# Writing out by hand the instruction order of a mixture of experts on three engines

## The chip, the cores and the metric

The kernel runs on one core of one Trainium2 chip. The metric is the device time of one execution in microseconds (us). A core has five engines that run side by side and wait for one another through semaphores: TensorE (PE in the profile; PEld are its weight loads), VectorE (DVE), ScalarE (ACT), GpSimd (POOL) and SyncE (SP). SP and POOL issue the data transfers here.

## The reference

Three layers follow one another on 2304 tokens of width 512: a windowed attention, a dense gated MLP, and a noisy top-2 mixture of 8 experts. The change touches the third alone:

```python
for e in range(E):                      # E = 8, F = 1024
    for k in range(2):
        mask = top2[:, k] == e
        h = np.maximum(x[mask] @ w1[e], 0.0)
        out[mask] += top2_w[mask, k, None] * (h @ w2[e])
```

## The kernel before

**Precision.** Every float32 operand of a large product is split into a high part (rounded to the matmul's type) and a low part (the rest). A product is three matmuls: high x high, high x low, low x high. A split is `Seven.split`: a copy on ScalarE writes the high part, then a subtraction on VectorE writes the low part. Weights come raw from HBM into one of three buffers `wst` and are split on the chip.

**An expert's tokens.** The tokens of an expert are 608 rows (`CW`) in 5 blocks (`CAP`). `gather(e, j)` fetches the rows of block j by an indirect DMA on POOL's queue into a tile `xo3` (two buffers). `gt(e, j, bank)` turns it with 4 transposes on TensorE; ScalarE copies the result into `xr`, and POOL copies the rows' weights into `wcol`.

**The first product** of experts 1 to 7 is `Seven.p1(e, i)` for i = 0 to 3, each for two of the 8 column blocks of `w1[e]`. It is a scheme of seven products (P1 to P7) on quarters of the operands instead of eight. `sums` makes four sums of quarters on VectorE (L1164 to L1167) and `operands(0..5)` split quarters and sums. Weights go through the same: `prep` takes the next job from the list `jobs`. A job ("w1", e, i) makes four differences on VectorE (L1142 to L1145) and four splits; a job ("w2", e, i) is one split of two column blocks of `w2[e]`. `load` issues the raw loads of the next jobs.

Each product is 6 matmuls (L1186). P1, P6 and P5 add up in one bank A. P1's result is needed alone as well, so ScalarE copies it to a bank B_ (L1199) before P6 may add to A; the copies C (L1203) and D_ (L1207) follow P6 and P5 in the same way, and `us` takes a copy of P7 (L1201). VectorE adds `us` to A (u0, L1208) and to C (u1, L1211). `out` finishes a quarter: an eviction with Relu on ScalarE (L1195), then its low part on VectorE (L1196).

**The second product** `p2(e, j)` is 24 matmuls (L315 to L317) for block j. VectorE then weights the result and adds it to the rows fetched from `out` by `prev(e, j)` (L970), and POOL scatters the rows back. Expert 0 is done by other functions, in part while the MLP still runs; the late half of its first product, `p1(0, f, (1,))` for 8 column blocks f (L932), and its blocks 3 and 4 of p2 stand at the start of this phase.

**What sets the order.** Instructions are written as a program; a scheduler orders them on each engine with a timeline of its own, by readiness and priority, and may move an instruction ahead of earlier ones. Within a region `tc.manual_schedule(engines=...)` the engines named issue in the order written; the others are left to the scheduler. Before, no such region covers the experts from `sv = Seven()` on.

Of the kernel before, what the change touches and what calls it, by code (L numbers as in the profile page):

```python
# [9 lines left out]
F32 = mybir.dt.float32  # L10
# [19 lines left out]
def tile_alibi_window_attention__swiglu__noisy_top2_moe(  # L30
# [33 lines left out]
    CAP = 5  # L64
# [13 lines left out]
    def bank(i):  # L78
        return psum.tile([128, 512], F32, name=f"b{i}", tag=f"b{i}")
# [222 lines left out]
    def place1(n):  # L302
        return main.tile([128, 2, 2, NU], F32R, name="wu", bufs=3)
# [594 lines left out]
    def gather(e, j):  # L898
        g = j >= EARLY
        if e == 0 and e not in XG:  # L900
            XG[e] = new_xt(e)
        x = wpool[3].tile([128, RW], F32, name="xo3", bufs=2) if e else wpool[1].tile([128, RW], F32, name="xo", bufs=2)
        GB[e, j] = x
        col = e * SB + j
        r = nrow(j)
        nc.gpsimd.indirect_dma_start(out=x[0:r], out_offset=None,  # L906
                                     in_=x2d[0:GRP[-1][0], :] if (e, g) == (0, False) else x2d,
                                     in_offset=bass.IndirectOffsetOnAxis(ap=R["g"][0:r, col:col + 1], axis=0))

    def gt(e, j, t):  # L910
        x, r = GB[e, j], nrow(j)
        for c in range(KC):
            nc.tensor.transpose(t[:, c * 128:c * 128 + r], x[0:r, c * 128:(c + 1) * 128], ident[0:r, 0:r])  # L913
        tv = t.rearrange("p (c s) -> p c s", c=KC)[:, :, 0:r]
        if e:
            nc.scalar.activation(sv.xr[:, :, j * 128:j * 128 + r], tv, AF.Copy)
        else:
            d = [XG[e][:, s, :].rearrange("p (c s) -> p c s", c=KC)[:, :, j * 128:j * 128 + r] for s in range(2)]
            nc.scalar.activation(d[0], tv, AF.Copy)
            nc.vector.tensor_sub(d[1], tv, f32(d[0]))  # L920
        nc.gpsimd.tensor_copy(wcol[0:r, e * CAP + j:e * CAP + j + 1], x[0:r, DM + e:DM + e + 1])
# [147 lines left out]
    class Seven:  # L1069
# [3 lines left out]
        def __init__(self):  # L1073
            self.xr = wpool[3].tile([128, KC, CW], F32, name="xr")
            n = 2 * HS
            s = wpool[3].tile([128, 4 * n], F32, name="xs")
            self.s = [s[:, i * n:(i + 1) * n].rearrange("p (c t) -> p c t", c=2) for i in range(4)]
            u = wpool[3].tile([128, 2 * HS], F32, name="us")
            self.u = [u[:, 0:HS], u[:, HS:]]
            self.t = hB[:, PB * DM:PB * DM + 1024].rearrange("p (o k f) -> p o k f", o=4, k=2)  # L1080
            z = NF2 * CW
            self.wb = [([hT[:, i, z:z + 512] for i in range(2)], [hT[:, i, z + 512:z + 768] for i in range(2)])]
            self.wa, self.w2, self.w2t = [], {}, None
            self.jobs = []
            for e in range(1, E):
                self.jobs += [("w1", e, i) for i in range(4)] + [("w2", e, i) for i in range(4)]
            self.jobs = ([j for j in self.jobs if j[:2] == ("w1", 1)][:3] +
                         [j for e in range(1, E) for j in
                          [("w1", e, 3)] + [("w2", e, i) for i in range(4)] + [("w1", e + 1, i) for i in range(3) if e + 1 < E]])
            self.nl = self.nj = 0  # L1090
            self.raw = {}

        def open(self):
# [34 lines left out]
            p, b = self.wb[i % 3]  # L1128
            return a, [x.rearrange("p (o k f) -> p o k f", o=2, k=2) for x in p], [x.rearrange("p (k f) -> p k f", k=2) for x in b]

        def prep(self, n=1):
            for _ in range(n):
                if self.nj == len(self.jobs):
                    return
                self.load(self.nj + 1)
                what, e, i = self.jobs[self.nj]
                r = self.raw.pop(self.nj)
                self.nj += 1
                if what == "w1":
                    a, b, c = w = self.w1_operands((e - 1) * 4 + i)  # L1140
                    t = self.t
                    nc.vector.tensor_sub(t[:, 0], r[:, 0:2, 1], r[:, 0:2, 0])  # L1142
                    nc.vector.tensor_sub(t[:, 1], r[:, 2:4, 1], t[:, 0])
                    nc.vector.tensor_sub(t[:, 2], r[:, 2:4, 1], r[:, 0:2, 1])
                    nc.vector.tensor_sub(t[:, 3], r[:, 2:4, 0], t[:, 1])  # L1145
                    self.split([a[:, s, 0:2].rearrange("p o k f -> p (o k) f") for s in range(2)], r[:, :, 0])
                    self.split([a[:, s, 2:4] for s in range(2)], t[:, 0:2])
                    self.split(b, t[:, 2:4])
                    self.split(c, r[:, 2:4, 1])
                    self.w2["w1", e, i] = w  # L1150
                else:
                    if i < 3:
                        t = place1(0)
                    else:
                        t = self.w2t
                    self.split([t[:, :, s, :] for s in range(2)], r)
                    for u in range(2):
                        self.w2[e, 2 * i + u] = t[:, u]
                self.load(self.nj + 2)

        def sums(self):
            x, s = self.xr, self.s
# [26 lines left out]
        def p1(self, e, i):  # L1189
            A, Z, B_, C, D_ = (bank(x)[:, 0:HS] for x in ((6, 7, 0, 1, 4), (2, 3, 5, 6, 7), (0, 1, 2, 3, 4), (5, 6, 7, 0, 1))[i])  # L1190
            lo, hi = slice(0, HS), slice(HS, CW)

            def out(ps, f, sl):
                d = h2[0][:, f, sl]
                nc.scalar.activation(d, ps, AF.Relu)  # L1195
                nc.vector.scalar_tensor_tensor(h2[1][:, f, sl], ps, 0.0, f32(d), op0=OP.max, op1=OP.subtract)  # L1196

            self.product(e, i, "P1", A, True)
            nc.scalar.activation(B_, A, AF.Copy)  # L1199
            self.product(e, i, "P7", Z, True)  # L1200
            nc.scalar.activation(self.u[1], Z, AF.Copy)  # L1201
            self.product(e, i, "P6", A, False)
            nc.scalar.activation(C, A, AF.Copy)  # L1203
            self.product(e, i, "P2", B_, False)
            out(B_, i, lo)
            self.product(e, i, "P5", A, False)
            nc.scalar.activation(D_, A, AF.Copy)  # L1207
            nc.vector.tensor_tensor(self.u[0], A, self.u[1], op=OP.add)  # L1208
            out(self.u[0], 4 + i, hi)
            self.product(e, i, "P4", C, False)  # L1210
            nc.vector.tensor_tensor(self.u[1], C, self.u[1], op=OP.add)  # L1211
            out(self.u[1], i, hi)
            self.product(e, i, "P3", D_, False)
            out(D_, 4 + i, lo)

    sv = Seven()
    for f in range(NF2):
        p1(0, f, (1,))
        if f == 3:
            sv.prep()  # L1220
    sv.open()
    sv.prep()
    for j in range(2):
        gather(1, j)
    for j in range(EARLY, CAP):
        prev(0, j)
        p2(0, j)
        if j == EARLY:
            for i in range(2):
                gt(1, i, bank(6 + i % 2))  # L1230
            for i in range(2, CAP):
                gather(1, i)
    for j in range(2, CAP):
        gt(1, j, bank(6 + j % 2))
        if j == 2:
            sv.operands(0)
    sv.sums()
    for i in range(1, 6):
        sv.operands(i)
    sv.prep()  # L1240
    for e in range(1, E):
        for i in range(4):
            sv.p1(e, i)
            sv.prep(2 if i == 0 else 1)
            if i == 1:
                for j in range(CAP):
                    prev(e, j)
            if i == 2 and e + 1 < E:
                for j in range(2):
                    gather(e + 1, j)  # L1250
        more = e + 1 < E
        for j in range(CAP):
            if more and j == 0:
                for i in range(2):
                    gt(e + 1, i, bank(6 + i))
                    gather(e + 1, 2 + i)
            p2(e, j)
            if not more:
                continue
            if j == 0:  # L1260
                for i in (2, 3):
                    gt(e + 1, i, bank(6 + i % 2))
                gather(e + 1, 4)
                sv.operands(0)
                sv.prep()
            if j == 1:
                gt(e + 1, 4, bank(6))
                sv.sums()
                sv.operands(5)
            if j == 2:  # L1270
                sv.operands(1)
                sv.operands(2)
                sv.operands(3)
                sv.operands(4)
            if j == 3:
                sv.prep(2)
    w3p_cm.__exit__(None, None, None)
    w2p_cm.__exit__(None, None, None)

# [71 lines left out]
```

## Time and profile before

| | us |
|---|---|
| median of 3 runs | 1099.27 |
| the runs | 1099.27, 1099.96, 1095.89 |
| the profiled execution's own time | 1095.33 |
| span of the profiled execution | 1093.2 |

The span is from the first to the last instruction of the profiled execution; 2.1 us of its time lie outside. The expert phase that the change touches is the last 420 us of it, from about 671 us on. The rows below show times in us from the start of the span; durations called mean are in ns.

### The profile page before, as it was taken

How to read it: one execution, taken by the hardware profiler on the slowest of the kernel's cores; microseconds unless marked ns; L12 is line 12 of the kernel's file. 1: busy time of each engine (PE TensorE's matmuls, PEld its weight loads, DVE VectorE, ACT ScalarE, POOL GpSimd, SP SyncE). 2: the span in 40 equal slices, each digit the busy share in tenths (PEclk: the TensorE clock that was granted, in tenths of full speed). 3: DMA queues.
4: the chain of work that ended last, by engine and by line, in shares of the span. 5: the costliest groups of instructions: out<-in, count | busy, mean ns of one | idle time of the engine just before them, and what ended most of it. 6: DMA issues, size and time to landing. Idle time of an engine off the chain costs nothing.

```text
span 1093.2 us, 18434 instructions
## 1 busy us (share of the span) xinstructions
PE 1053.2 (96%) x6830; PEld 895.5 (82%) x6830; DVE 679.3 (62%) x1518; ACT 560.3 (51%) x1255; POOL 343.8 (31%) x324
## 2 busy tenths in 40 slices
PE   6889999999999999999999999989999999999996
PEld 5667778889988777788998888878888888888895
DVE  6778963576630477316785365866767686858551
ACT  6877864455532355434542242655655564646440
POOL 7300002121233333141368304425242423332211
PEclk9899999999999999999999999999999999999998
DMA  9698755233372333241332413545445453535211
GB/s 209 182 248 261 246 175 175 71 86 91 91 242 97 106 86 106 71 155 40 99 97 97 142 53 105 163 149 153 136 136 155 129 161 123 161 118 169 92 47 45
DMA packets 140258, 143.91 MB, mean 132 GB/s; under 512 B 66510, under 2 KB 109518, under 8 KB 140160
## 3 DMA queue, kind: packets, MB, share of 16 engines
q1 hardware_dynamic: 129776, 113.09, 34.9%
q0 software_dynamic: 9184, 29.26, 8.7%
q8 instruction: 56, 0.92, 0.4%
q10 hardware_dynamic: 1200, 0.30, 0.1%
q14 instruction: 42, 0.34, 0.1%
HBM read 113.84 MB, written 28.91 MB: 131 GB/s over the span
## 4 chain that ended last, share of the span: by engine, by line
PE 83%; DVE 6%; ACT 5%; DMA 3%; issue 2%; ACTq 0%; POOL 0%; POOLq 0%; DVEq 0%
PE b L315 21%; PE b L316 20%; PE b L317 20%; PE b L1186 7%; PE b L510 3%; PE b L932 2%; DMA wst<-in_moe_w_dram 2%; PE b L480 2%; PE b L463 2%; PE b L913 2%; ACT wu L1116 1%; DVE wu L1117 1%; PE b L378 1%; DVE hTa L1196 1%; PE b L698 1%
## 5 line engine op out<-in xcount | busy, mean ns | idle before, releaser
L296 POOL TENSOR_TENSOR wu<-wst,wu 128x1024 fp32r<-128x1024 f32 x54 | 129.8, 2406 | 265.2 <-ACT wu L295 246.5
L315 PE MATMUL b<-xT,wu 128*128 128x320 f32 (+1 forms) x576 | 199.8, 351 | 4.6 <-ACT xT L525 4.5
L316 PE MATMUL b<-xT,wu 128*128 128x320 f32 (+1 forms) x576 | 198.0, 344 | 0.1
L317 PE MATMUL b<-xT,wu 128*128 128x320 f32 (+1 forms) x576 | 197.1, 343 | 0.0
L315 PE MATMUL b<-wu,hTa 128*128 128x512 f32 (+1 forms) x482 | 191.8, 400 | 0.0
L316 PE MATMUL b<-wu,hTa 128*128 128x512 f32 (+1 forms) x482 | 190.3, 395 | 0.0
L317 PE MATMUL b<-wu,hTa 128*128 128x512 f32 (+1 forms) x482 | 188.8, 396 | 0.0
L1186 PE MATMUL b<-xT,wu 128*128 128x304 f32 x834 | 127.3, 304 | 10.6 <-ACT b L1199 9.8
L1186 PEld LDWEIGHTS b<-xT,wu 128*128 128x128 f32 x834 | 118.8, 188 | 14.8 <-ACT b L1199 11.6
L295 ACT ACTIVATE wu<-wst 128x1024 fp32r<-128x1024 f32 x80 | 84.3, 1056 | 79.7 <-PE b L317 63.7
L315 PEld LDWEIGHTS b<-xT,wu 128*128 128x128 f32 x576 | 107.8, 188 | 16.8 <-ACT xT L525 5.8
L316 PEld LDWEIGHTS b<-xT,wu 128*128 128x128 f32 x576 | 109.3, 190 | 9.8 <-issue 1.6
L317 PEld LDWEIGHTS b<-xT,wu 128*128 128x128 f32 x576 | 109.2, 190 | 9.0 <-issue 1.5
L315 PEld LDWEIGHTS b<-wu,hTa 128*128 128x128 f32 (+1 forms) x482 | 88.9, 185 | 21.6 <-DVE hTa L1196 1.0
L317 PEld LDWEIGHTS b<-wu,hTa 128*128 128x128 f32 (+1 forms) x482 | 88.9, 184 | 21.1 <-issue 0.3
L316 PEld LDWEIGHTS b<-wu,hTa 128*128 128x128 f32 (+1 forms) x482 | 89.1, 185 | 20.7 <-issue 0.6
L610 DVE TENSOR_TENSOR hTa<-sg,hTa 128x320 fp32r<-128x320 f32 (+1 forms) x54 | 69.0, 1283 | 23.0 <-ACT hTa L609 22.9
L970 DVE SCALAR_TENSOR_TENSOR hTb<-b,wcol,hTb 128x512 f32<-128x512 f32 (+1 forms) x35 | 26.2, 748 | 89.6 <-PE b L317 56.7
L906 POOL DMA_INDIRECT xo<-x2d,gib x37 | 42.6, 1152 | 118.4 <-PE b L1186 70.1
L974 POOL DMA_INDIRECT out_dram<-hTb,sib x39 | 46.8, 1200 | 96.3 <-DVE hTb L970 85.6
L424 ACT ACTIVATE sx<-sx,mn 128x192 f32<-128x192 f32 (+2 forms) x126 | 53.6, 427 | 41.4 <-DVE mn L421 40.9
L1117 DVE TENSOR_TENSOR wu<-wst,wu 128x1024 fp32r<-128x1024 f32 (+2 forms) x65 | 56.7, 880 | 25.1 <-ACT wu L1116 25.0
(240 smaller groups left out, 1841.2 us busy)
## 6 DMA issues: line engine op xcount, KB each, us to landing
wst<-wscr SPq DMA_DIRECT2D x54, 512.0 KB, 3.3
wst<-in_moe_w_dram SPq DMA_DIRECT2D x36, 512.0 KB, 3.9
wst<-in_moe_w_dram SPq DMA_DIRECT2D x56, 256.0 KB, 3.3
wscr<-wst SPq DMA_DIRECT2D x18, 512.0 KB, 3.2
cs<-in_moe_w_gate_dram SPq DMA_DIRECT2D x12, 512.0 KB, 5.1
cs<-in_moe_w_val_dram SPq DMA_DIRECT2D x12, 512.0 KB, 6.4
cs<-in_moe_w_out_dram SPq DMA_DIRECT2D x12, 512.0 KB, 5.6
x2d<-xT SPq DMA_DIRECT2D x18, 256.0 KB, 3.1
```

Source lines behind the costliest of these rows:

```text
L295: nc.scalar.activation(o[0], s, AF.Copy)
L296: self.eng(n).tensor_sub(o[1], s, f32(o[0]))
L315: nc.tensor.matmul(ps, st(0), mv(0), start=first, stop=False, skip_group_check=True)
L316: nc.tensor.matmul(ps, st(0), mv(1), start=False, stop=False, skip_group_check=True)
L317: nc.tensor.matmul(ps, st(1), mv(0), start=False, stop=last, skip_group_check=True)
L424: a = nc.scalar.activation(x, x, AF.Exp, scale=-1.0, bias=mn[:, i:i + 1], accum_out=sm[:, i:i + 1])
L510: mm.append(nc.tensor.matmul(x[64 * h:64 * h + 64, (j - j0) * 64:(j - j0 + w) * 64], wt, st["pt"][kk, h ^ sw, c:c + 64 * w], start=(n == 0 ...
L610: nc.vector.tensor_sub(hh(1, f, sl), t, f32(hh(0, f, sl)))
L906: nc.gpsimd.indirect_dma_start(out=x[0:r], out_offset=None, in_=x2d[0:GRP[-1][0], :] if (e, g) == (0, False) else x2d, in_offset=bass.Indi ...
L974: s = nc.gpsimd.indirect_dma_start(out=out, out_offset=bass.IndirectOffsetOnAxis(ap=R["s"][0:r, col:col + 1], axis=0), in_=x, in_offset=No ...
L1117: nc.vector.tensor_sub(o[1], src, f32(o[0]))
L1186: nc.tensor.matmul(ps, w[k][:, c], x[:, m, c], start=first and c == 0 and k + m == 0, stop=c == 1 and k == 1, skip_group_check=True)
```

## The change

The last part of the function, from `sv = Seven()` on, is put into one manual region for TensorE, ScalarE and VectorE, and its statements are rearranged.

- Weight jobs become lists of pieces: `prep` only appends closures to `todo`, and `some(n)` writes out the next n. A w1 job has four pieces (the four differences and the first split; three more splits); a w2 job has two, one for each column block, where it was one split of double width. The next loads are issued behind a job's last piece.
- In `p1` one piece is written behind the copies of P7 and P6 and one behind the first `out`. P3 and its `out` of calls 1 and 2 move behind the next call's copy B_.
- The order of the jobs changes: w2's first two, then w1's last, then w2's last two. Jobs of the next expert's w1 are written behind the blocks 1, 2 and 3 of p2.
- `second(e)` holds p2 of expert e with the transposes, sums and operands of expert e + 1 between.
- For expert 1 the first w1 job runs in pieces during `p1(0, f)`; the second and third are written whole behind p2(0, 4) and its operands.
- The five gathers of an expert are issued together, behind the five `prev` in call 1 of `p1`; four of them go into the memory of the sums (`xs`), the fifth into `xo3`, now one buffer.

```diff
-        x = wpool[3].tile([128, RW], F32, name="xo3", bufs=2) if e else wpool[1].tile([128, RW], F32, name="xo", bufs=2)
+        x = (sv.g[j] if j < 4 else wpool[3].tile([128, RW], F32, name="xo3")) if e else wpool[1].tile([128, RW], F32, name="xo", bufs=2)
...
+            self.g = [s[:, i * RW:(i + 1) * RW] for i in range(4)]
...
-            self.jobs = ([j for j in self.jobs if j[:2] == ("w1", 1)][:3] +
+            self.jobs = ([("w1", 1, i) for i in range(3)] +
                          [j for e in range(1, E) for j in
-                          [("w1", e, 3)] + [("w2", e, i) for i in range(4)] + [("w1", e + 1, i) for i in range(3) if e + 1 < E]])
+                          [("w2", e, 0), ("w2", e, 1), ("w1", e, 3), ("w2", e, 2), ("w2", e, 3)] + [("w1", e + 1, i) for i in range(3) if e + 1 < E]])
...
+        def prep(self):
+            if self.nj == len(self.jobs):
+                return
+            self.load(self.nj + 1)
+            what, e, i = self.jobs[self.nj]
+            r = self.raw.pop(self.nj)
+            self.nj += 1
+            if what == "w1":
+                a, b, c = w = self.w1_operands((e - 1) * 4 + i)
+                t = self.t
+                def first():
                     nc.vector.tensor_sub(t[:, 0], r[:, 0:2, 1], r[:, 0:2, 0])
                     nc.vector.tensor_sub(t[:, 1], r[:, 2:4, 1], t[:, 0])
                     nc.vector.tensor_sub(t[:, 2], r[:, 2:4, 1], r[:, 0:2, 1])
                     nc.vector.tensor_sub(t[:, 3], r[:, 2:4, 0], t[:, 1])
                     self.split([a[:, s, 0:2].rearrange("p o k f -> p (o k) f") for s in range(2)], r[:, :, 0])
+                self.todo += [first, lambda: self.split([a[:, s, 2:4] for s in range(2)], t[:, 0:2]),
+                              lambda: self.split(b, t[:, 2:4]), lambda: self.split(c, r[:, 2:4, 1])]
+                self.w2["w1", e, i] = w
+            else:
+                t = place1(0) if i < 3 else self.w2t
+                self.todo += [lambda u=u: self.split([t[:, u, s, :] for s in range(2)], r[:, u]) for u in range(2)]
+                for u in range(2):
+                    self.w2[e, 2 * i + u] = t[:, u]
+            f = self.todo.pop()
+            self.todo.append(lambda: (f(), self.load(self.nj + 2)))
+        def some(self, n):
+            while n and self.todo:
+                f = self.todo.pop(0)
+                f()
+                n -= 1
...
+            def last():
+                self.product(e, i, "P3", D_, False)
+                self.rest = lambda: out(D_, 4 + i, lo)
             self.product(e, i, "P1", A, True)
             nc.scalar.activation(B_, A, AF.Copy)
+            if i in (2, 3):
+                self.last()
+            self.rest()
             self.product(e, i, "P7", Z, True)
             nc.scalar.activation(self.u[1], Z, AF.Copy)
+            self.some(1)
             self.product(e, i, "P6", A, False)
             nc.scalar.activation(C, A, AF.Copy)
+            self.some(1)
             self.product(e, i, "P2", B_, False)
             out(B_, i, lo)
+            self.some(1)
             self.product(e, i, "P5", A, False)
             nc.scalar.activation(D_, A, AF.Copy)
             nc.vector.tensor_tensor(self.u[0], A, self.u[1], op=OP.add)
...
-            self.product(e, i, "P3", D_, False)
-            out(D_, 4 + i, lo)
+            if i in (0, 3):
+                last()
+                if i == 3:
+                    self.rest()
+                    self.rest = lambda: None
+            else:
+                self.last = last

     sv = Seven()
+    for j in range(CAP):
+        gather(1, j)
+    by_hand = tc.manual_schedule(engines={mybir.EngineType.PE, mybir.EngineType.Activation, mybir.EngineType.DVE})
+    by_hand.__enter__()
     for f in range(NF2):
         p1(0, f, (1,))
         if f == 3:
             sv.prep()
+        sv.some(1)
+    sv.some(9)
     sv.open()
...
+    def second(e):
+        n = e + 1
+        more = n < E
+        if more:
+            gt(n, 0, bank(6))
+            gt(n, 1, bank(7))
+        j0 = 0 if e else EARLY
+        p2(e, j0, 0, 4)
+        if more:
+            gt(n, 2, bank(6))
+            gt(n, 3, bank(7))
+        p2(e, j0, 4, 8)
+        if more:
+            sv.operands(0)
+            gt(n, 4, bank(6))
+            sv.sums()
+            for i in (3, 2):
+                sv.operands(i)
+        p2(e, j0 + 1)
+        if more:
+            for i in (1, 5, 4):
+                sv.operands(i)
+            sv.prep()
+            sv.some(9)
+        for j in range(j0 + 2, CAP):
+            p2(e, j)
+            if more and j < 4:
+                sv.prep()
+                sv.some(9)
+        if more and e == 0:
+            sv.prep()
+            sv.some(9)
     for j in range(EARLY, CAP):
         prev(0, j)
+    second(0)
...
     for e in range(1, E):
         for i in range(4):
+            for _ in range(2 if i == 0 else 1):
+                sv.prep()
             sv.p1(e, i)
-            sv.prep(2 if i == 0 else 1)
             if i == 1:
                 for j in range(CAP):
                     prev(e, j)
+                if e + 1 < E:
+                    for j in range(CAP):
+                        gather(e + 1, j)
...
+        sv.some(9)
+        second(e)
+    by_hand.__exit__(None, None, None)
```

## Rows read from the trace of the kernel before

**Rows 1.** The page: busy time of two engines, share of the span, instructions.

```profile
PE 1053.2 (96%) x6830; PEld 895.5 (82%) x6830; DVE 679.3 (62%) x1518; ACT 560.3 (51%) x1255; POOL 343.8 (31%) x324
```

**Rows 2.** Windows: time, then busy us (x instructions) of PE, PEld, DVE, ACT, POOL; PEclk, DMA share, GB/s.

```profile
670.73:724.52 53.79, 50.12 (x338) 44.82 (x336) 46.36 (x92) 36.36 (x76) 21.59 (x24) 1.00 0.57 164
754.02:780.30 26.28, 24.78 (x173) 23.74 (x171) 21.83 (x48) 20.07 (x47) 6.55 (x7) 1.00 0.56 171
754.02:809.90 55.88, 54.38 (x309) 47.23 (x308) 39.57 (x75) 31.06 (x63) 18.74 (x20) 1.00 0.47 142
...
977.00:1033.22 56.22, 54.39 (x310) 47.05 (x308) 39.49 (x75) 31.07 (x63) 17.07 (x16) 1.00 0.44 132
1033.22:1056.17 22.95, 22.82 (x164) 22.57 (x163) 13.78 (x26) 14.88 (x35) 6.02 (x6) 1.00 0.34 103
```

**Rows 3.** The chain of work that ended last: start, us, instruction and count.

```profile
681.93 2.67 PE b L932 x24
...
686.47 0.44 PE b L913 x4
...
1033.38 19.22 PE b L1186 x138
...
1066.45 0.46 PE b L317 x2
```

**Rows 4.** Waits from 680 us on: who waited for whom; us, times, longest.

```profile
PEld b L1186 <- ACT b L1199: 11.6, 7, 2.6
...
PE b L913 <- DMA xo<-x2d,gib: 0.4, 1, 0.4
```

**Rows 5.** Timeline of one wait in expert 2: start, us, instruction.

```profile
769.10 0.40 ACT L1195 ACTIVATE hTa<-b 128x304 fp32r<-128x304 f32 x1
769.40 0.45 ACT L1195 ACTIVATE hTa<-us 128x304 fp32r<-128x304 f32 x1
...
769.75 0.41 ACT L1199 ACTIVATE b<-b 128x304 f32<-128x304 f32 x1
...
770.22 1.68 PEld L1186 LDWEIGHTS b<-xT,wu 128*128 128x128 f32 x12 [1.64 <-ACT b L1199]
```

**Rows 6.** Groups by shape from 680 us on: busy us, mean ns, idle before, releasers.

```profile
L1117 DVE TENSOR_TENSOR wu<-wst,wu 128x1024 fp32r<-128x1024 f32 x28 | 34.3, 1225 | 21.4 <-ACT wu L1116 21.4
...
L1195 ACT ACTIVATE hTa<-us 128x304 fp32r<-128x304 f32 x56 | 25.4, 454 | 19.2 <-DVE us L1208 10.4 <-DVE us L1211 8.7
...
L1117 DVE TENSOR_TENSOR wu<-hTb,wu 128x512 fp32r<-128x512 f32 x36 | 24.5, 684 | 3.6 <-ACT wu L1116 3.6
...
L1117 DVE TENSOR_TENSOR xT<-xs,xT 128x608 fp32r<-128x608 f32 x28 | 21.3, 782 | 0.0
...
L970 DVE SCALAR_TENSOR_TENSOR hTb<-b,wcol,hTb 128x512 f32<-128x512 f32 x28 | 21.0, 749 | 81.8 <-PE b L317 48.9 <-issue 28.5 <-POOL wcol L921 4.4
...
L1199 ACT ACTIVATE b<-b 128x304 f32<-128x304 f32 x28 | 11.4, 410 | 15.5 <-PE b L1186 15.3 <-DVE hTa L1196 0.2
```

**Rows 7.** Timeline around u0 in expert 2's first product: start, us, instruction.

```profile
774.38 0.69 DVE L1117 TENSOR_TENSOR wu<-hTb,wu 128x512 fp32r<-128x512 f32 x1 [0.44 <-ACT wu L1116]
...
774.99 0.47 DVE L1208 TENSOR_TENSOR us<-b,us 128x304 f32<-128x304 f32 x1
775.37 0.41 DVE L1142 TENSOR_TENSOR hTb<-wst 128x256 f32<-128x256 f32 x1
775.49 0.46 ACT L1195 ACTIVATE hTa<-us 128x304 fp32r<-128x304 f32 x1 [0.28 <-DVE us L1208]
```

**Rows 8.** The page, DMA issues: count, KB each, median us from issue to landing.

```profile
wst<-in_moe_w_dram SPq DMA_DIRECT2D x56, 256.0 KB, 3.3
```

**Rows 9.** Windows, as rows 2: an early stretch, and the end of the span.

```profile
32.73:39.55 6.82, 5.83 (x41) 5.30 (x40) 6.73 (x20) 4.90 (x17) 2.27 (x4) 0.50 1.04 345
1080.00:1085.00 5.00, 4.97 (x22) 3.19 (x20) 0.27 (x1) 0.00 (x0) 0.98 (x1) 1.00 0.16 56
...
1089.00:1093.00 4.00, 0.00 (x0) 0.00 (x0) 0.00 (x0) 0.00 (x0) 0.00 (x0) 0.50 0.01 4
```

More of the change, by code (lines that the diff above doesn't have):

```diff
@@ L1083, in __init__ @@
             self.wa, self.w2, self.w2t = [], {}, None
-            self.jobs = []
-            for e in range(1, E):
-                self.jobs += [("w1", e, i) for i in range(4)] + [("w2", e, i) for i in range(4)]
-            self.jobs = ([j for j in self.jobs if j[:2] == ("w1", 1)][:3] +
+            self.jobs = ([("w1", 1, i) for i in range(3)] +
                          [j for e in range(1, E) for j in
-                          [("w1", e, 3)] + [("w2", e, i) for i in range(4)] + [("w1", e + 1, i) for i in range(3) if e + 1 < E]])
+                          [("w2", e, 0), ("w2", e, 1), ("w1", e, 3), ("w2", e, 2), ("w2", e, 3)] + [("w1", e + 1, i) for i in range(3) if e + 1 < E]])
             self.nl = self.nj = 0
+            self.rest = lambda: None
+            self.todo = []
             self.raw = {}
@@ L1129, in w1_operands @@
             return a, [x.rearrange("p (o k f) -> p o k f", o=2, k=2) for x in p], [x.rearrange("p (k f) -> p k f", k=2) for x in b]
[L1131 to L1141, printed above, removed]
+        def prep(self):
[9 more added lines that the diff above has]
+                def first():
                     nc.vector.tensor_sub(t[:, 0], r[:, 0:2, 1], r[:, 0:2, 0])
@@ L1146, in prep @@
                     self.split([a[:, s, 0:2].rearrange("p o k f -> p (o k) f") for s in range(2)], r[:, :, 0])
[L1147 to L1159, printed above, removed]
+                self.todo += [first, lambda: self.split([a[:, s, 2:4] for s in range(2)], t[:, 0:2]),
[13 more added lines that the diff above has]
+                n -= 1
         def sums(self):
@@ L1212, in p1 @@
             out(self.u[1], i, hi)
-            self.product(e, i, "P3", D_, False)
-            out(D_, 4 + i, lo)
+            if i in (0, 3):
+                last()
+                if i == 3:
+                    self.rest()
+                    self.rest = lambda: None
+            else:
+                self.last = last
     sv = Seven()
+    for j in range(CAP):
+        gather(1, j)
+    by_hand = tc.manual_schedule(engines={mybir.EngineType.PE, mybir.EngineType.Activation, mybir.EngineType.DVE})
+    by_hand.__enter__()
     for f in range(NF2):
@@ L1220, in tile_alibi_window_attention__swiglu__noisy_top2_moe @@
             sv.prep()
+        sv.some(1)
+    sv.some(9)
     sv.open()
-    sv.prep()
-    for j in range(2):
-        gather(1, j)
+    def second(e):
[30 more added lines that the diff above has]
+            sv.some(9)
     for j in range(EARLY, CAP):
         prev(0, j)
[L1227 to L1240, printed above, removed]
+    second(0)
     for e in range(1, E):
         for i in range(4):
+            for _ in range(2 if i == 0 else 1):
+                sv.prep()
             sv.p1(e, i)
-            sv.prep(2 if i == 0 else 1)
             if i == 1:
@@ L1247, in tile_alibi_window_attention__swiglu__noisy_top2_moe @@
                     prev(e, j)
[L1248 to L1276, printed above, removed]
+                if e + 1 < E:
[4 more added lines that the diff above has]
+    by_hand.__exit__(None, None, None)
     w3p_cm.__exit__(None, None, None)
```

## The prediction

> **What bounds the kernel now.** I read the page's busy shares first: TensorE is busy for 96% of the span and VectorE for 62% [rows 1], so time can be gained only where TensorE stands still, or lost where it is made to. Next come the windows of the expert phase [rows 2]. From 754.0 on the work of one expert repeats five times, the first taking 55.88 us and the last 56.22. I compare each stretch with what its matmuls need. The chain of waits gives their pace: a first-product matmul (L1186) starts every 19.22 / 138 = 0.139 us, one of the second product (p2) every 0.23 us, one of expert 0's late first product (L932) every 0.111 us, and a gathered block costs four transposes, 0.44 us [rows 3]. The first product of an expert is 4 calls of `Seven.p1` with 7 products of 6 matmuls: 168 x 0.139 = 23.35 us. Expert 2's takes 26.28 us with one block of transposes inside, so 26.28 - 0.44 - 23.35 = 2.5 us are waits; I take that for each of experts 2 to 6. Expert 7's has 162 of its matmuls in 22.95 us: 0.4 us of waits. The stretch from expert 0's late first product to expert 1's second takes 53.79 us; its 96 + 48 + 168 matmuls and six blocks of transposes need 10.7 + 11.0 + 23.35 + 2.6 = 47.7, so 6.1 are waits. The second products run without a gap worth naming. The list of waits names the cause: TensorE waits for ScalarE's copy at L1199 seven times, 11.6 us in all, 2.6 us at most [rows 4]. The timeline of one such wait shows how: two evictions (L1195) run on ScalarE directly ahead of the copy, the copy ends at 770.16, and TensorE resumes at 770.22 [rows 5]. This copy (B_ = A) must be made after product P1 and before P6 adds to the same bank; only P7, 6 x 0.139 = 0.83 us, lies between.
>
> So the limit is TensorE's own pace plus short waits for ScalarE's copies. If every wait of experts 1 to 7 went away, the gain would be 6.1 + 5 x 2.5 + 0.4 = 19 us; that is the most this change can bring.
>
> **What the new order does, part by part.** I lay the same durations into the new order, each engine strictly in that order. An instruction on VectorE or ScalarE starts about 0.08 us before the one ahead of it ends (774.38 + 0.69 against 774.99), and an eviction that needs u0 starts 0.50 us after u0 does [rows 7]. So I count 0.60 us for a 512-wide subtraction, 1.14 for 1024, 0.70 for 608, 0.33 for 256, 0.67 for an accumulation (L970), 0.37 for an eviction out of `us` and 0.33 for a copy, from their durations [rows 6, 7].
>
> *The handover from expert 0 to 1.* Both orders reach 671.0, the first matmul of p1(0, f), alike. From there TensorE has 96 x 0.111 = 10.7 us of it, 48 x 0.23 = 11.0 us of p2(0,3) and p2(0,4), and five blocks of transposes, 2.2 us. One new wait falls in p1(0): the first piece of w1(1,0) puts four subtractions and a 1024-wide one ahead of the eviction that frees one of its two banks. These are 1.44 (0.33 each, and 0.12 for the second, which reads the first's result) + 1.14 us, against 1.33 us for the one call in between, so I count 1.2 us. TensorE then starts p1(1,0) at 671.0 + 10.7 + 1.2 + 2.2 + 11.0 = 696.1, and wants P6 two products later, at 697.8. But the splits of w1(1,1) and w1(1,2) now stand ahead of the copy B_ = A on ScalarE, and behind the accumulation of p2(0,4) on VectorE. VectorE comes to that accumulation at about 696.7: p2(0,3) is out at 690.4, and its accumulation, the 1216-wide operand (twice a 608), four sums and two operands take 0.67 + 1.4 + 6 x 0.70. Then follow 0.67 and three operand subtractions (3 x 0.70), to 699.5; w1(1,1) whole, 1.44 + 1.14 + 2 x 0.60 + 0.33 = 4.1, to 703.6; and the first two subtractions of w1(1,2), to 704.5. Only then can ScalarE do its last three splits (0.54, a wait of 0.1, 0.54, 0.30), to 706.0, and the copy, to 706.4. P6 waits 8.6 us. Before, these splits are partly done in VectorE's and ScalarE's gaps while p1(0) and p2(0) run; the new order has the gaps, but may not use them.
>
> *The boundaries between two calls of p1.* In the new order a call ends on VectorE with u0, its low part, u1, its low part, and each low part waits for ScalarE's eviction. The chain from u0 to the next call's P6 is 0.50 (eviction of u0), 0.48 (low part), 0.385 (u1 follows), 0.50 (eviction of u1), 0.37 (the copy B_ follows it), 0.41 and 0.05 (the copy and TensorE's start): 2.7 us. TensorE comes to that P6 five products after P5's start, at 4.17 us, and P5 is over at about 1.03. So u0 may come 0.45 us after P5's end; what it lags beyond that TensorE stands still. After call 1 the lag is worst, because w1(e,3)'s first piece is in it. VectorE can begin at 1.7 us after the call's copy B_ starts, and then has 0.60 + 1.44 + 1.14 + 0.385 + 0.60 = 4.2 us before u0, which so starts at 5.9; P5 is over at 3.3. The lag is 2.6 and the wait 2.15 us. After call 0 (two 512-wide pieces and a low part ahead of u0) the lag is about 1.0 and the wait 0.5; after call 2 it is 0.8 and 0.35. Together 3.0 us, and each restart costs 0.1 us more, since the second matmul after the wait at 770.22 starts late by as much: 3.3 us for each expert.
>
> *What costs nothing.* A w2 split in two halves takes VectorE 2 x 0.60 for 1.14 us; VectorE has 16 us free in an expert's 55.9 [rows 2], and where it does not, this is in the lags above. The five gathers in one place stand behind five row loads on GpSimd's queue, which is busy for 18.7 us of 55.9; the one wait of TensorE for a gather today is 0.4 us [rows 4]. If that cover failed, TensorE would wait at the transposes. The weight loads land 3.3 us after issue [rows 8], and a buffer is free a whole call or p2 (over 5 us) before its next use; if not, ScalarE would wait up to 3.3 us.
>
> *TensorE's clock.* After its last matmul the granted clock falls: 1.00 up to 1085, 0.50 from 1089 on, which is the 1.2 GHz level; an early stretch at 0.50 lasted 6.82 us [rows 9]. TensorE would stand still for 8.6 us at expert 1, so I expect the lower level there too. Matmuls at half pace for 6.82 us lose 3.4; nothing is the other bound; part is covered by engines that are late anyway, so I take 2. The Trainium skill, "TensorE: Matmul & The Clock Gate", "What's actually happening", says that the throttled level is the default and activity releases it; the end of this trace agrees (0.50 when idle). Without such a fall the sum would be 2 us lower.
>
> **The sum.** p2(1,0) begins at 696.1 + 8.6 + 23.35 + 2 x 0.44 + 3.0 + 0.4 = 732.3 against 724.52 [rows 2], with one block of transposes more behind it: 7.4 us later. Experts 2 to 6: 3.3 - 2.5 = 0.8 us each, 4.0. Expert 7: 3.3 - 0.4 = 2.9. Clock: 2. In all 16.3 us. The profiled execution took 1095.3 us for a span of 1093.2; 1095.3 + 16.3 = 1111.6. The median of the runs is 4 us above that execution, and two of three runs lie there, so by them it would be 1115.5. I say **1113 us**; its own range is 1105 to 1121.
>
> **Rivals.**
> *The order works.* If the pieces behind the copies let each copy start at once, the boundaries cost nothing and the handover no more than today. Experts 2 to 6 give back 5 x 2.5 us and expert 7 0.4: 1099.3 - 12.9 = 1086. It decides from the point at which u0 lags under 0.45 us. For it: ScalarE's L1199 copies lose their evictions ahead in the calls' middle. Against it: the sums on VectorE above. The Trainium skill, "TensorE: Matmul & The Clock Gate", "Architectural detail: the array is 16× 32×32, not 1× 128×128", says that ScalarE's and VectorE's queues are strictly first in, first out, which is what the walk supposes; in the timeline above, the copy runs behind two evictions and does not overtake [rows 5]. Chance 0.09.
> *Handover lost, steady state won.* The 8.6 us at expert 1 come, but the boundaries cost nothing: 7.4 - 3.0 - 0.3 + 2 - 12.9 = -7 at most, or about -1 if they cost a quarter: 1092 to 1098. Chance 0.13.
> *The cover fails.* If all three boundaries were as late as the worst (2.15 us), an expert would cost 6.8, not 3.3: 7 x 3.5 = 24 us more, 1137. It needs loads or VectorE to be later than any row shows. Chance 0.06.
> *No effect.* If the engines' order were this one already, nothing would move. The timeline excludes it: behind u0 (774.99) VectorE runs a first-piece subtraction (L1142) at 775.37, where the new order has u0's low part [rows 7].
>
> The forecast holds 0.72. Measurements of this kernel cannot tell less than 0.5%, 5.5 us, from no change. The first rival is all faster; the second is half faster, half same; of the forecast, a few in a hundred reach down to within 0.5%. So faster 0.15, same 0.10, slower 0.75. The range, 1096 to 1122, leaves out the first rival and a third of the second below (0.13) and the third above (0.06).
>
> **What would show it.** Right: a wait of about 8 us of TensorE on L1199's copy near 698, a clock of 0.50 behind it, and three waits on the same copy for each expert, the longest (about 2 us) in the third call; expert periods near 56.7 us; expert 7's first product over 26 us. Wrong: periods below 55 us, or no wait above 3 us ahead of 710. The handover is the term on which the sign hangs most; the lag of u0 in call 1 is next.

## The result and the profile after

The changed kernel takes 1107.53 us (median of 4 runs, 1106.8 to 1108.1) against 1098.51 us for the kernel before (4 runs): a ratio of 1.0084, 95% interval 1.0063 to 1.0106. It is 0.8% slower. Its profiled execution took 1107.09 us for a span of 1105.1.

The page: busy time, and the 40 slices of TensorE and of its clock.

```profile
PE 1055.2 (95%) x6830; PEld 900.2 (81%) x6830; DVE 690.6 (62%) x1546; ACT 560.3 (51%) x1283; POOL 345.1 (31%) x324
...
PE   6889999999999999999999999699999999999997
...
PEclk9899999999999999999999999899999999999999
```

TensorE is busy for 2 us more than in [rows 1] and the span is 11.9 us longer. One slice in the middle, near 700 us, shows a 6, and the clock of the same slice an 8. The windows take that place apart; then follow experts 2, 3 and 6, each from the first matmul of its first product to the same of the next expert, and expert 7's first product (columns as in [rows 2]).

```profile
697.20:705.86 8.66, 0.31 (x3) 0.06 (x1) 8.59 (x19) 4.90 (x11) 7.59 (x6) 0.73 0.35 104
701.20:711.44 10.24, 5.58 (x22) 5.58 (x23) 8.19 (x17) 6.24 (x14) 8.25 (x9) 0.50 0.79 256
...
762.33:818.37 56.04, 54.10 (x310) 47.37 (x308) 41.44 (x79) 31.16 (x67) 20.20 (x20) 1.00 0.46 139
818.37:874.41 56.04, 54.10 (x310) 47.38 (x308) 41.45 (x79) 31.18 (x67) 20.37 (x20) 1.00 0.45 141
986.69:1042.74 56.05, 54.09 (x309) 47.37 (x308) 41.45 (x79) 31.18 (x67) 11.60 (x10) 1.00 0.39 121
1042.74:1068.88 26.14, 24.18 (x170) 23.44 (x169) 18.45 (x37) 16.97 (x42) 6.02 (x6) 1.00 0.38 114
```

TensorE does nearly nothing from 697.2 to 705.9, while VectorE is busy for 8.59 of these 8.66 us. The clock stands at 0.50, the 1.2 GHz level, from 701.2 for 10.24 us. Experts 2 to 6 now all take the same 56.04 us (expert 5, where two small waits differ, 56.24); before, they took 55.5 to 56.3.

The list of waits from 680 us on (the copy B_ is now L1208, the matmul L1191, the eviction L1200, u0 L1223):

```profile
ACT hTa L1200 <- DVE us L1223: 30.9, 28, 1.7
PEld b L1191 <- ACT b L1208: 27.0, 21, 8.6
...
PE b L1191 <- ACT b L1208: 21.8, 21, 8.4
```

Where [rows 4] had 7 waits of TensorE on this copy, there are 21: three for each of seven experts (the first of expert 1's is the one near 700 us). The timeline around the longest shows what stands ahead of the copy.

```profile
695.67 0.99 PE L1191 MATMUL b<-xT,wu 128*128 128x304 f32 x6
...
696.61 0.74 DVE L972 TENSOR_SCALAR hTb<-b,wcol 96x512 f32<-96x512 f32 x1
...
699.38 0.41 DVE L1144 TENSOR_TENSOR hTb<-wst 128x256 f32<-128x256 f32 x1
...
702.98 0.42 DVE L1144 TENSOR_TENSOR hTb<-wst 128x256 f32<-128x256 f32 x1
...
703.89 1.30 ACT L1116 ACTIVATE wu<-hTb 128x512 fp32r<-128x512 f32 x2 [1.48 <-DVE hTb L1145]
...
705.10 0.40 ACT L1116 ACTIVATE wu<-wst 128x256 fp32r<-128x256 f32 x1
...
705.40 0.40 ACT L1208 ACTIVATE b<-b 128x304 f32<-128x304 f32 x1
...
705.86 1.38 PE L1191 MATMUL b<-xT,wu 128*128 128x304 f32 x4 [8.35 <-ACT b L1208]
```

VectorE comes to the weighting of p2(0,4) at 696.61, begins the differences of w1(1,1) at 699.38 and those of w1(1,2) at 702.98; ScalarE stands 1.48 us in its queue, waiting for these, makes the last splits, and only then the copy that TensorE has wanted since 697.4.

The second fence is the boundary from call 1 to call 2 in expert 2, which answers to [rows 7]:

```profile
769.88 0.41 ACT L1208 ACTIVATE b<-b 128x304 f32<-128x304 f32 x1
...
771.55 0.69 DVE L1117 TENSOR_TENSOR wu<-wst,wu 128x512 fp32r<-128x512 f32 x1 [0.42 <-ACT wu L1116]
...
772.16 0.42 DVE L1144 TENSOR_TENSOR hTb<-wst 128x256 f32<-128x256 f32 x1
...
773.62 0.69 DVE L1117 TENSOR_TENSOR wu<-wst,wu 128x512 fp32r<-128x512 f32 x1
774.23 0.47 DVE L1201 SCALAR_TENSOR_TENSOR hTa<-b,hTa 128x304 fp32r<-128x304 f32 x1
774.61 0.68 DVE L1117 TENSOR_TENSOR wu<-hTb,wu 128x512 fp32r<-128x512 f32 x1
775.21 0.47 DVE L1223 TENSOR_TENSOR us<-b,us 128x304 f32<-128x304 f32 x1
...
775.71 0.46 ACT L1200 ACTIVATE hTa<-us 128x304 fp32r<-128x304 f32 x1 [1.70 <-DVE us L1223]
776.20 0.47 DVE L1201 SCALAR_TENSOR_TENSOR hTa<-us,hTa 128x304 fp32r<-128x304 f32 x1 [0.53 <-ACT hTa L1200]
776.60 0.47 DVE L1226 TENSOR_TENSOR us<-b,us 128x304 f32<-128x304 f32 x1
777.10 0.46 ACT L1200 ACTIVATE hTa<-us 128x304 fp32r<-128x304 f32 x1 [0.93 <-DVE us L1226]
777.46 0.41 ACT L1208 ACTIVATE b<-b 128x304 f32<-128x304 f32 x1
...
777.92 0.41 PE L1191 MATMUL b<-xT,wu 128*128 128x304 f32 x1 [1.46 <-ACT b L1208]
```

From u0's start (775.21) to TensorE's (777.92) it is 2.71 us: eviction, low part, u1, eviction, copy, each waiting for the one ahead of it on the other engine. VectorE reaches u0 only after two pieces of w1(2,3), the first of which begins with the four differences.

### The profile page after: what moved, and what is told of

It is laid out like the page before. It is cut to its first block, busy times and chain, and to the rows that moved or that the text cites. A ratio compares the mean times of both kernels' runs of the same rounds, so it can differ in the third digit from the quotient of the medians.

```text
span 1105.1 us, 18329 instructions
## 1 busy us (share of the span) xinstructions
PE 1055.2 (95%) x6830; PEld 900.2 (81%) x6830; DVE 690.6 (62%) x1546; ACT 560.3 (51%) x1283; POOL 345.1 (31%) x324
## 5 line engine op out<-in xcount | busy, mean ns | idle before, releaser
L1191 PE MATMUL b<-xT,wu 128*128 128x304 f32 x834 | 128.9, 308 | 21.8 <-ACT b L1208 21.8
L1191 PEld LDWEIGHTS b<-xT,wu 128*128 128x128 f32 x834 | 120.3, 191 | 27.9 <-ACT b L1208 27.0
L974 POOL DMA_INDIRECT out_dram<-hTb,sib x39 | 44.4, 1139 | 98.6 <-DVE hTb L970 64.0
L1117 DVE TENSOR_TENSOR wu<-wst,wu 128x512 fp32r<-128x512 f32 x93 | 61.6, 662 | 21.7 <-ACT wu L1116 21.4
L1116 ACT ACTIVATE wu<-wst 128x512 fp32r<-128x512 f32 x93 | 55.4, 600 | 0.0
```

The source lines that it names most:

```text
L974: s = nc.gpsimd.indirect_dma_start(out=out, out_offset=bass.IndirectOffsetOnAxis(ap=R["s"][0:r, col:col + 1], axis=0), in_=x, in_offset=No ...
L1116: nc.scalar.activation(o[0], src, AF.Copy)
L1117: nc.vector.tensor_sub(o[1], src, f32(o[0]))
L1191: nc.tensor.matmul(ps, w[k][:, c], x[:, m, c], start=first and c == 0 and k + m == 0, stop=c == 1 and k == 1, skip_group_check=True)
```

## The experiments

Three costs were to be told apart: the two weight jobs ahead of the copy at the handover; the ping-pong behind u0 at each boundary; the first piece of w1(e,3) in call 1. The rivals are the region itself and the gathers. The table gives all kernels at once. "Expert 2" is when the first matmul of expert 2's first product starts in the profiled execution, "an expert" the mean distance of that place from expert 2 to 7 (five of them). Each ratio is to runs of the kernel before taken beside that kernel's own (their medians: 1098.51 us for the changed kernel; 1097.54 for splits early, low parts last, two gathers and TensorE alone; 1098.57 for the other four). All compute the whole reference.

| kernel | median us (runs) | ratio to before, 95% | expert 2 | an expert |
|---|---|---|---|---|
| before | 1098.51 (4) | 1 | 754.02 | 55.84 |
| after | 1107.53 (4) | 1.0063 to 1.0106 | 762.33 | 56.08 |
| splits early | 1098.03 (10) | 0.9990 to 1.0014 | 753.00 | 56.05 |
| low parts last | 1096.48 (10) | 0.9976 to 1.0000 | 761.33 | 54.31 |
| differences early | 1103.70 (5) | 1.0030 to 1.0064 | 764.89 | 55.31 |
| the first two | 1090.08 (6) | 0.9898 to 0.9935 | 756.20 | 54.30 |
| all three | 1083.81 (5) | 0.9846 to 0.9888 | 755.30 | 53.31 |
| two gathers | 1125.66 (4) | 1.0225 to 1.0265 | 768.03 | 58.73 |
| region for TensorE alone | 1104.79 (8) | 1.0043 to 1.0074 | 757.15 | 56.24 |
| no region | 1104.94 (4) | 1.0032 to 1.0069 | 753.37 | 59.03 |

Without a region the scheduler puts the first 7 matmuls of each first product ahead of the last block of p2 (expert 2's at 746.83); the table has the time of the eighth.

**The splits of w1(1,1) and w1(1,2) early.** They are written in `second(0)` between the transposes and the halves of p2(0,3).

```diff
             gt(n, 1, bank(7))
+        if e == 0:
+            sv.prep()
+            sv.some(9)
...
             gt(n, 3, bank(7))
+        if e == 0:
+            sv.prep()
+            sv.some(9)
...
-            sv.prep()
-            sv.some(9)
+            if e:
+                sv.prep()
+                sv.some(9)
...
-        if more and e == 0:
-            sv.prep()
-            sv.some(9)
```

> Splits of w1(1,1) and w1(1,2) written ahead of the operands of expert 1, in the stretch where VectorE waits for p2(0,3). If the handover's wait comes from these splits standing ahead of the first bank copy, the 8.5 us gap near 697 shrinks to about 2 us (some is given back because the operands start later), the granted clock stays at 1.00 there, and the time falls by 6 to 8 us against the changed kernel (1107.5), to about 1100, the level of the kernel before; the gaps inside experts 2 to 7 stay at 0.5, 1.6 and 0.3 us. If the loss at the handover comes from something else (gathers, transposes, loads), the gap stays above 6 us.

Windows of this kernel: the wait at the handover, then from p1(1,0) to the second block of p2(1).

```profile
697.30:698.51 1.21, 0.31 (x3) 0.06 (x1) 1.21 (x2) 1.21 (x4) 0.96 (x1) 1.00 0.00 0
695.69:730.67 34.98, 32.11 (x213) 29.91 (x212) 23.68 (x48) 23.65 (x54) 15.54 (x15) 1.00 0.50 148
```

The distance of 8.66 us between two matmuls is now 1.21, the clock stays at 1.00, and the median falls by 9.5 us, to that of the kernel before. The same stretch takes 44.34 us in the changed kernel, from the window

```profile
695.67:740.01 44.34, 34.29 (x214) 32.40 (x212) 30.76 (x63) 27.56 (x61) 14.03 (x14) 0.88 0.45 142
```

so 9.36 us less, of which 8.66 - 1.21 = 7.45 are the wait, and 1.9 are left for the lower clock and for small waits that differ. An expert stays at 56.05: the handover and the boundaries are two separate costs. By the medians the first alone (9.5 us) is the whole loss against before (9.0); between the profiled executions it is 9.5 of 11.9 us, and the 2.4 that are left come from the boundaries (from expert 2 on 3.4 us more than before, less 1.0 by which expert 2 now starts earlier).

**Low parts last.** Both evictions and u1 come ahead of both low parts.

```diff
-            out(self.u[0], 4 + i, hi)
+            d0, d1 = h2[0][:, 4 + i, hi], h2[0][:, i, hi]
+            nc.scalar.activation(d0, self.u[0], AF.Relu)
...
-            out(self.u[1], i, hi)
+            nc.scalar.activation(d1, self.u[1], AF.Relu)
+            for f, u, d in ((4 + i, self.u[0], d0), (i, self.u[1], d1)):
+                nc.vector.scalar_tensor_tensor(h2[1][:, f, hi], u, 0.0, f32(d), op0=OP.max, op1=OP.subtract)
```

> The two low parts at the end of a call are written behind u1, so that u1 no longer waits for ScalarE's eviction of u0. If the chain u0, eviction, low part, u1, eviction, copy sets the gaps at the call boundaries, the gaps after calls 0 and 2 vanish and the one after call 1 falls from 1.6 to under 1 us: 1.5 to 2 us less for each of 7 experts, 10 to 13 us in all, to 1095 to 1098; the gap of 8.5 us at 697 stays. If VectorE's load alone sets the gaps (the same instructions in any order), nothing changes by more than 3 us.

The timeline of the same boundary, call 1 to 2 in expert 2:

```profile
773.67 0.47 DVE L1223 TENSOR_TENSOR us<-b,us 128x304 f32<-128x304 f32 x1
...
774.17 0.46 ACT L1225 ACTIVATE hTa<-us 128x304 fp32r<-128x304 f32 x1 [1.69 <-DVE us L1223]
774.24 0.47 DVE L1227 TENSOR_TENSOR us<-b,us 128x304 f32<-128x304 f32 x1
...
775.11 0.41 ACT L1208 ACTIVATE b<-b 128x304 f32<-128x304 f32 x1
...
775.57 0.69 PE L1191 MATMUL b<-xT,wu 128*128 128x304 f32 x3 [0.73 <-ACT b L1208]
```

The copy starts 1.44 us after u0 instead of 2.25. The waits after calls 0 and 2 are gone, the one after call 1 is 0.9 us (1.63 before the edit), and an expert takes 1.8 us less. The handover stays at 8.66 us, with 10.24 us at 0.50 behind it.

**Differences early.** The four differences of w1(e,3) are written at the end of call 0 and left out of the job's first piece.

```diff
                 def first():
+                    if i < 3:
+                        self.differences(r)
...
             sv.p1(e, i)
+            if i == 0:
+                sv.load(sv.nj + 1)
+                sv.differences(sv.raw[sv.nj])
```

> The changed kernel with one edit: the four differences of w1(e,3) are written at the end of call 0 instead of in call 1. If VectorE's work ahead of u0 sets the gap after call 1, this gap falls by 0.7 to 1.4 us (from 1.6) in each of 7 experts, the two others stay, and the time falls by 5 to 9 us to 1099 to 1103. If the gap comes from ScalarE or TensorE, nothing changes.

The distance after call 1 falls from 1.77 to 1.00 us, those after calls 0 and 2 stay at 0.62 and 0.46, and an expert takes 0.77 less. So VectorE's work ahead of u0 sets the lag of call 1, as the walk had it. Of the 1.44 us that the four take, 0.77 comes off, since VectorE still does them behind the copy of call 1, in part in time in which it stood idle. The median of 1103.7 lies just above the 1099 to 1103 that were expected; where p1(0) adds to it stands at the end of the next part.

**The first two together, and all three.**

> Splits of w1(1,1) and w1(1,2) early and low parts last, together. If the two waits are separate costs, their gains add up: 1107.5 - 9.5 - 11 = 1087, about 1% faster than the kernel before (1097.5). If they share a cause or TensorE meets another limit behind them, the time is 1092 or more.

> All three edits. With the low parts last, the gap after call 1 is 0.9 us; without the four differences ahead of u0 it should fall to 0.2 or less: 4 to 5 us under the version with two edits, 1082 to 1084. If that gap has another cause, the same time as with two edits.

With two edits a distance of 1.04 us is left for each expert, after call 1; with all three nothing. The 1090.1 of the two lies between the 1087 of plain addition and the 1092 that stood for a shared cause. Place by place the gains do add up (1.22 us at the handover, 54.30 for an expert); what is missing stands in p1(0). The page, then windows of experts 3 and 4 and of expert 7's first product, of the kernel with all three:

```profile
PE 1051.6 (97%) x6830; PEld 900.5 (83%) x6830; DVE 691.8 (64%) x1546; ACT 561.1 (52%) x1283; POOL 345.6 (32%) x324
```

```profile
808.61:861.92 53.31, 53.31 (x310) 47.36 (x309) 41.36 (x79) 31.18 (x67) 19.91 (x20) 1.00 0.48 149
861.92:915.22 53.30, 53.30 (x309) 47.35 (x308) 41.42 (x79) 31.22 (x67) 19.35 (x20) 1.00 0.48 147
1021.84:1045.80 23.96, 23.86 (x169) 23.42 (x168) 18.47 (x37) 17.02 (x42) 6.06 (x6) 1.00 0.39 124
```

TensorE is busy for all 53.31 us of an expert: that is what the work needs, and 56.08 - 53.31 = 2.77 us is what the three boundaries cost in the changed kernel, 55.84 - 53.31 = 2.53 what the waits cost before. This version beats the kernel before by 1.3% (ratio 0.9867). In these two kernels and in the one with early differences, p1(0) has three distances of 0.54, 1.58 and 1.04 us where the changed kernel has one of 0.84. In these two p1(0) also starts 2.7 us later (673.3 against 670.65), with early differences 1.4; this delay is there from the first 105 us of the program on, which no edit touches. So p1(1,0) starts some 5 us later in these two (700.6 against 695.67). What causes this was not followed, and whether it can be won is not shown.

**Two gathers at a time.** The buffers and places of the gathers as before; the order of the rest as in the changed kernel.

```diff
-        x = (sv.g[j] if j < 4 else wpool[3].tile([128, RW], F32, name="xo3")) if e else wpool[1].tile([128, RW], F32, name="xo", bufs=2)
+        x = wpool[3].tile([128, RW], F32, name="xo3", bufs=2) if e else wpool[1].tile([128, RW], F32, name="xo", bufs=2)
...
+            gather(n, 2)
...
+            gather(n, 3)
...
+            gather(n, 4)
```

> The gathers as before: two buffers, two gathers ahead and three behind the transposes that free a buffer; everything else as changed. If the five gathers at once are among the causes of the loss, the time falls below 1107 by several us. By the theory of the queues they cost nothing and are needed: transposes 2 and 3 come 2.8 us after 0 and 1, and a gather needs 1.2 us of issue and some 2.5 to land, so TensorE waits 1 to 2 us at each of two places for each of 7 experts: 1115 to 1130.

Waits of TensorE from 680 us on:

```profile
PE b L913 <- DMA xo<-x2d,gib: 12.1, 13, 1.4
```

It is 18 us slower than the changed kernel. The transposes now wait for the rows, 13 times, where no such wait is in the changed kernel's list; with it an expert takes 2.65 us more. The five gathers at once are thus no part of the loss, and this order of p2 needs them.

**The region for TensorE alone, and no region.**

```diff
-    by_hand = tc.manual_schedule(engines={mybir.EngineType.PE, mybir.EngineType.Activation, mybir.EngineType.DVE})
+    by_hand = tc.manual_schedule(engines={mybir.EngineType.PE})
```

```diff
-    by_hand = tc.manual_schedule(engines={mybir.EngineType.PE, mybir.EngineType.Activation, mybir.EngineType.DVE})
-    by_hand.__enter__()
...
-    by_hand.__exit__(None, None, None)
```

> Only TensorE's order is written by hand; ScalarE and VectorE are left to the scheduler with the same statements. If the loss is ScalarE's and VectorE's strict order, the gap at 697 falls under 4 us and the time falls by 4 us or more, to 1095 to 1103. If TensorE's own order (calls of p1 no longer overlapping) is the cause, gaps on the copy B_ stay and the time stays at 1105 to 1110 or above.

> The changed kernel's statements, pieces and gathers without the region: the scheduler orders all three engines. If the region's strict order is the whole loss, this is as fast as the kernel before or faster (1090 to 1098). If the statements' arrangement itself (pieces, gathers, order of the jobs) costs time, it stays above 1100.

With ScalarE and VectorE left to the scheduler the handover costs three distances of 2.24, 1.76 and 0.88 us instead of 8.66; the first two are waits for operand splits on VectorE, not for the copy. But an expert costs as much as in the changed kernel, and the time falls by 2.7 us where 4 or more were expected. The timeline of expert 2's first copy B_, in call 0, with the region for TensorE alone:

```profile
759.17 0.63 ACT L1116 ACTIVATE wu<-wst 128x512 fp32r<-128x512 f32 x1 [3.44 <-DMA wst<-in_moe_w_dram]
759.71 0.41 ACT L1208 ACTIVATE b<-b 128x304 f32<-128x304 f32 x1
...
760.17 1.93 PE L1191 MATMUL b<-xT,wu 128*128 128x304 f32 x12 [1.18 <-ACT b L1208]
```

The scheduler puts a split ahead of the copy whose raw weights come late: ScalarE stands for 3.44 us and TensorE behind it for 1.18. Without any region expert 2 starts earlier than in the kernel before (753.37 against 754.02), but an expert then takes 59.03 us, with distances of 2.27 us and the clock at 0.50 three times. That execution is the slowest of its four (1109.71 us); experts 2 and 6, in which the clock stayed at 1.00, still take 58.0 and 58.6. So leaving the order to the scheduler does not undo the loss; the same statements in its hands lose it elsewhere. Why it did 3.2 us better per expert with the statements of before was not followed.

## Why the prediction came out as it did

The sign, the place and the mechanism were right; the sum of 16.3 us was measured as 11.9 between the two profiled executions (last matmul at 1096.85 against 1084.97), and the time is 1107.5 instead of 1113.

- *The handover.* Predicted: p1(1,0) at 696.1, P6 after 8.6 us of waiting at 706.5. Measured: 695.67 and 705.86, with 8.66 from one matmul to the next, 8.5 of it wait. VectorE reached the accumulation of p2(0,4) at 696.61, predicted 696.7. Taking the two jobs away from this place removed 9.5 us of time: shown.
- *The clock.* Predicted 2 us, measured 1.9 by the difference of the two stretches above, as a remainder. The matmuls themselves show 2.3: from 706.28 to 711.35 one starts every 0.253 us instead of every 0.14 (with the splits early a wait of 0.46 us after call 0, which the changed kernel does not have there, takes the rest). The low stretch was longer (10.24 us) than the 6.82 of [rows 9], by which I had sized it, and 4.7 us of it lay inside the wait, where it costs nothing. The rule that the prediction takes from the Trainium skill, "TensorE: Matmul & The Clock Gate", "What's actually happening", fits this trace (the clock fell at 701.2, while TensorE stood still).
- *The boundaries.* Predicted waits 0.5, 2.15 and 0.35, with restarts 3.3 us per expert. Measured 0.48, 1.63 and 0.32 (distances of 0.62, 1.77 and 0.46 less the pace of 0.14), with restarts 2.77. The chain from u0 to TensorE was predicted 2.7 and is 2.71. So experts 2 to 6 cost 5 x (56.08 - 55.84) = 1.2 us more and not 4.0, and what lies behind expert 7's start 2.4 instead of 2.9.
- *The term that was mis-sized.* In three places the working takes the first split of a w1 job as 1024 wide, 1.14 us on VectorE. The trace shows it at 512 (773.62 in the second timeline), so 0.60. The 1024-wide row of [rows 6] is of the w2 splits alone: its count of 28 is four a piece for seven experts. This one width is 0.54 us too much in p1(0) (1.2 predicted, 0.7 measured), in w1(1,1) at the handover (4.1 predicted; 702.98 - 699.38 = 3.6 measured), and in call 1 of seven experts (2.15 against 1.63): 9 x 0.54 = 4.9, and 16.3 - 4.9 = 11.4 stands beside the 11.9 measured.
- *The level.* The 1113 was set between two sums because the profiled execution of before lay 3 to 4 us under its median. That of the changed kernel lies 0.4 under its own, so the medians differ by 9.0 and the profiled executions by 11.8. A sum made against one execution carries its luck.
- *The rivals.* "The order works" did not come, since u0 lags in every call; its price was about right: the version without lags takes 1083.8, it was given 1086. "Handover lost, steady state won" did not come, but is what "low parts last" does (1096.5; it was given 1092 to 1098). "The cover fails" did not come in the changed kernel: neither loads nor gathers made TensorE wait. It came in the other orders, through the gathers (two at a time) and through the loads (TensorE alone). "No effect" did not come: TensorE waits 21 times on the copy instead of 7, and the interval of the ratio, 1.0063 to 1.0106, lies above 1.

## What to carry to other kernels

When an order is written by hand, walk each engine's queue up to the instruction that the bounding engine waits for next, and ask what stands ahead of it that is needed only later: here two weight jobs ahead of one copy of 0.4 us cost 9.5 us, and moving them by a few statements gave all of it back. Where two engines pass work to and fro behind the bounding one, issue all that lies on that path first and the rest (here the low parts) after it. Before multiplying a duration from a grouped row, check by its count which operation of the code the row is.

## What the runs showed of the hardware

The clock fell to 0.50 not only behind the one long wait. With the region for TensorE alone it fell for 3.4 us though no two matmuls were more than 2.24 us apart; without a region it fell three times, each for 3.4 us, behind single distances of 2.27 and 2.28 us. With two gathers at a time it fell for 3.4 us at 859.5, behind distances of 1.62 and 1.01 us; the expert in which it did took 59.97 us, the four others 58.24 to 58.69. The windows with the region for TensorE alone:

```profile
697.20:703.10 5.90, 2.50 (x16) 2.00 (x15) 5.90 (x10) 3.07 (x6) 2.26 (x2) 1.00 0.45 134
703.10:706.50 3.40, 3.40 (x15) 3.40 (x15) 1.96 (x4) 2.48 (x6) 2.63 (x4) 0.50 0.79 222
```

In the kernel without a region, a row of a stretch behind which the clock did not fall, then one behind which it did, with the low stretch:

```profile
766.30:770.30 4.00, 2.03 (x14) 1.78 (x14) 4.00 (x11) 2.44 (x6) 3.09 (x4) 1.00 0.51 139
...
824.00:828.00 4.00, 2.03 (x14) 1.78 (x14) 4.00 (x11) 2.32 (x7) 3.08 (x4) 1.00 0.66 188
828.00:831.40 3.40, 3.40 (x16) 3.40 (x15) 2.22 (x7) 2.09 (x6) 0.44 (x1) 0.51 0.90 308
```

In both kernels TensorE was busy for about half of the stretch ahead (2.50 of 5.90 us, 2.03 of 4.00), and it runs the low stretch without a break, a matmul every 0.253 us instead of every 0.14. But the row from 766.30 has the same distance of 2.27 us and the same busy time, and behind it the clock stayed at 1.00, as it did behind one of 2.28 us at 1005.1. So these runs show that the clock can fall behind waits of this size, and not when it will. In the changed kernel the waits of 1.63 us left it at 1.00 each time. Small waits can thus cost more than their sum: in that expert of the two gathers at least 1.2 us more than in any of the four others.
